# Loading q and k of the first attention tiles with one transfer each instead of two, and re-timing the first weights

## Chip, cores, metric

One core of a Trainium2 chip. The metric is the device time of one execution in microseconds (us). The kernel before takes 225.16 us (median of 5 runs, 224.05 to 225.39).

## The reference, cut to what matters

```python
# q, k, v: (4 batches, 8 heads, 768 tokens, 64)
scores = scale * q @ k^T + bias      # bias: minus slope(head) times distance
keep   = key is one of the first 8 tokens, or at most 95 tokens behind the query
a      = softmax(where(keep, scores, -1e9))
x      = (a @ v), laid out as (3072 tokens, 512)
h      = x @ w_in                    # 512 x 2048
out    = (h - tanh(h)) @ w_out       # 2048 x 512
```

## The kernel before: the parts that matter

The work is cut into 24 tiles of 128 tokens. For each tile, attention (load k, q, v; cast; transpose; scores "S"; exp "E"; "AV"; normalise; transpose of x) is followed by the MLP in two layers, `m1` (w_in) and `m2` (w_out). All attention of a tile and all MLP work share TensorE (PE). A small list scheduler inside the kernel decides the order of the instructions on each engine from estimated durations; each engine then runs its own queue in order.

```python
    PE_B = 4                 # tiles whose bias is added by a matmul; later ones are masked by VectorE
    PE_T, PE_X = 10, 10      # tiles whose transposes run on TensorE; later ones by DMA
...
    def load(u, nm, src, dst):
        ...
        if u < PE_B and nm != "vf":          # k and q of tiles 0..3: rows of 8 tokens = 2 KB
            for a in range(2):               # two transfers of 64 partitions
                started(("ld", nm, u), nc.sync.dma_start(
                    out=dst[u][a * Dh : (a + 1) * Dh].rearrange("p t d -> p (t d)"),
                    in_=rows[a * NP : (a + 1) * NP].rearrange("h (k t) d -> k h (t d)", t=H),
                ))
        else:                                # v, and later tiles: pieces of 64 numbers = 256 B
            started(("ld", nm, u), nc.sync.dma_start(out=dst[u], in_=rows.rearrange("h p d -> p h d")))
...
    WARM = (1.4, 19.0)       # filler matmuls on a zero tile keep PE busy up to here
    T_LD, T_LD8 = 1.15, 0.7  # the scheduler's idea of 256 KB in 256 B and in 2 KB pieces
    before = [ ("t", 0), ("t", 1), ("t", 2), ("t", 3), ("in", 0), ("in", 1), ("in", 2), ("in", 3), ("out", 0), ...
    # the first weight load after tiles waits for the landing of the last tile's k: w_in 0 waits for k of tile 3
```

The four quarters of w_in are called w_in_97, 98, 99 and 100, those of w_out w_out_101 to 104.

The softmax here doesn't subtract the row's maximum and nothing guards it: scores larger than these inputs give would overflow.

Of the kernel before, what the change touches and what calls it, by code (L numbers as in the profile page):

```python
# [8 lines left out]
FP32 = mybir.dt.float32  # L9
# [7 lines left out]
def kernel(  # L17
# [11 lines left out]
    nc = tc.nc  # L29

    B, H, S, Dh = q.shape
    P = 128
    NQ = S // P
    NP = H // 2
# [10 lines left out]
    WJ = 4  # L45
    FJ = CF // WJ
    NV = 8
    PE_B = 4
    PE_T, PE_X = 10, 10
    HT = 3  # L50


    EARLY, EARLY2 = 6, 4
    groups = [[u] for u in range(EARLY)] + [[u, u + 1, u + 2] for u in range(EARLY, NU, HT)]
    group_of = {u: g for g, us in enumerate(groups) for u in us}

# [77 lines left out]
    gate_of = {}  # L134
    dmas = {}

    def started(key, i):
        dmas[key] = i
        g = gate_of.get(key)
        if g is not None:  # L140
            tc.add_manual_dep(
                i.ins, dmas[g].ins.name,
                mybir.DependencyInfo(mybir.DependencyClass.Sync, mybir.DependencyReason.DATA),
                reason="order of loads",
            )


    kf, qf, vf = {}, {}, {}
    kq = {}

    def load(u, nm, src, dst):
        b, i = u // NQ, u % NQ
        dst[u] = stpool.tile([P, H, Dh], FP32, name=nm)
        rows = src[b, :, i * P : (i + 1) * P, :]
        if u < PE_B and nm != "vf":


            for a in range(2):
                started(("ld", nm, u), nc.sync.dma_start(  # L159
                    out=dst[u][a * Dh : (a + 1) * Dh].rearrange("p t d -> p (t d)"),  # L160
                    in_=rows[a * NP : (a + 1) * NP].rearrange("h (k t) d -> k h (t d)", t=H),
                ))
        else:
            started(("ld", nm, u), nc.sync.dma_start(out=dst[u], in_=rows.rearrange("h p d -> p h d")))  # L164

    def load_w_in(j):
        w = DFF // WJ
# [5 lines left out]
    def cast(u, j, src, eng):  # L173
        if u not in kq:
            kq[u] = bpool.tile([P, 2, H * Dh], BF16, name="kq")
        t = src.pop(u)
        if u < PE_B:
            eng.tensor_copy(out=kq[u][:, j, :], in_=t.rearrange("p h d -> p (h d)"))  # L178
        else:
            eng.tensor_copy(  # L180
                out=kq[u][:, j, :].rearrange("p (c a d) -> p a c d", a=2, d=Dh),
                in_=t.rearrange("p (a c) d -> p a c d", a=2),
            )
# [7 lines left out]
    def a_T(u):  # L191
        tr[u] = ps_one.tile([P, 2, NP, P], BF16, name="one")
        for j in (1, 0):
            if u < PE_B:
                for t in range(H):
                    for a in range(2):
                        r = slice(a * Dh, (a + 1) * Dh)
                        nc.tensor.transpose(
                            tr[u][r, j].rearrange("r c f -> r (c f)")[:, t * Dh : (t + 1) * Dh],
                            kq[u][r, j, t * Dh : (t + 1) * Dh], ident[r, r],  # L200
                        )
                continue
            for p in range(NP):
                nc.tensor.transpose(tr[u][:, j, p, :], kq[u][:, j, p * P : (p + 1) * P], ident)  # L204

    def a_DT(u):
        qk[u] = kpool.tile([P, 2, NP, P], BF16, name="qk")
# [10 lines left out]
    def a_Te(u, j, e):  # L218
        if u not in qk:
            qk[u] = kpool.tile([P, 2, NP, P], BF16, name="qk")  # L220
        if u < PE_B:
            copy(e, out=qk[u][:, j].rearrange("r c (k t) -> r c k t", t=H),
                 in_=tr[u][:, j].rearrange("r c f -> r (c f)").rearrange(
                     "r (t k c) -> r c k t", t=H, c=NP))
        else:
            copy(e, out=qk[u][:, j], in_=tr[u][:, j])

# [133 lines left out]
    def store(u):  # L361
        nc.sync.dma_start(out=out[u * P : (u + 1) * P, :], in_=ots.pop(u))


    AHEAD = 6.0
    WARM = (1.4, 19.0)
    T_LD, T_LD8, T_ST, T_DT, T_DX = 1.15, 0.7, 0.7, 1.75, 0.9
    T_W = {"in": 3.15, "out": 2.65}
    before = [
        ("t", 0), ("t", 1), ("t", 2), ("t", 3), ("in", 0), ("in", 1), ("in", 2), ("in", 3), ("out", 0),  # L370
        ("out", 1), ("t", 4), ("out", 2), ("out", 3), ("t", 5), ("t", 6), ("t", 7),
    ]

    def landed(it):
        return ("ld", "vf", it[1]) if it[0] == "t" else it

    tiles = [it[1] for it in before if it[0] == "t"]
    for u in range(NU):
        if u not in tiles:
            gate_of["ld", "kf", u] = ("ld", "kf", tiles[-1])  # L380
            tiles.append(u)
    for n, it in enumerate(before):
        if n and it[0] != "t" and before[n - 1][0] == "t":
            gate_of[it] = ("ld", "kf", before[n - 1][1])
        elif n >= 2 and it[0] == "t" and before[n - 1][0] != "t":
            gate_of["ld", "kf", it[1]] = landed(before[n - 2])
    prev = None
    for it in before:
        if it[0] != "t":
# [17 lines left out]
    for u in tiles:  # L407
        for nm, src, dst in (("kf", k, kf), ("qf", q, qf), ("vf", v, vf)):
            key = ("ld", nm, u)
            op(key, SP, 0.55 if u >= PE_B or nm == "vf" else 0.8, lambda u=u, nm=nm, src=src, dst=dst: load(u, nm, src, dst),  # L410
               after=[gate_of.get(key), prev and ("issue", prev)], take=[nm], dma=T_LD if u >= PE_B or nm == "vf" else T_LD8)
            prev = key
    for u in range(NU):
        i = u % NQ
        e0 = DVE if u == 0 else POOL
        c0 = 0.5 if u == 0 else 0.62
        op(("ck", u), e0, c0, lambda u=u, e=e0: cast(u, 1, kf, nc.vector if e is DVE else nc.gpsimd),
           after=[("ld", "kf", u)], take=["kq"], give=["kf"], pri=-1)
        op(("cq", u), e0, c0, lambda u=u, e=e0: cast(u, 0, qf, nc.vector if e is DVE else nc.gpsimd),
           after=[("ld", "qf", u), ("ck", u)], give=["qf"], pri=-1)  # L420
        op(("cv", u), POOL, 0.62, lambda u=u: cast_v(u),
           after=[("ld", "vf", u), ("AV", u - NV + 1) if u >= NV else None,
                  ("V", (u - NV) // NQ * NQ + NQ - 2) if u >= NV else None], give=["vf"])
        go = [key for a, key in prog if a <= u - AHEAD]
        tdep = [("ck", u), ("cq", u), ("issue", ("T", u - 1)) if u else None, go[-1] if go else None]
        if u < PE_T:
            op(("T", u), PE, 0.7 if u < PE_B else 0.46, lambda u=u: a_T(u), after=tdep, take=["one"], give=["kq"])
            for j in (1, 0):
                op(("Te", u, j), (DVE, ACT), (0.5, 0.62), lambda e, u=u, j=j: a_Te(u, j, e), after=[("T", u)])
            op(("Te", u, 2), DVE, 0.0, lambda: None, after=[("Te", u, 0), ("Te", u, 1)], give=["one"])  # L430
        else:
            op(("T", u), SP, 1.2, lambda u=u: a_DT(u), after=tdep, give=["kq"], dma=T_DT)
        te = ("Te", u, 2) if u < PE_T else ("T", u)
        for o in (0, 1) if i else (0,):
            op(("S", u, o), PE, 0.69 if u < PE_B else 0.24, lambda u=u, o=o: a_S(u, o),
               after=[te, "bias" if u < PE_B else None, ("K", u - 1) if o and i >= 2 else None], take=["big"])
            op(("E", u, o), ACT, 1.03, lambda u=u, o=o: a_E(u, o), after=[("S", u, o)],
               take=["p%d" % o], give=["big"])
            if u >= PE_B:
                op(("M", u, o), DVE, 0.73, lambda u=u, o=o: a_M(u, o),  # L440
                   after=[("E", u, o), ("mk", H - 1)])
# [40 lines left out]
    def plan():  # L482
        bufs = {"big": 2, "one": 4, "mo": 3, "kf": 4, "qf": 4, "vf": 4, "kq": 3, "p0": 3, "p1": 3,
                "x": 3, "xT": 4, "g": 3, "th": 3, "ot": 4}
        avail = {n: [0.0] * c for n, c in bufs.items()}
        free = {PE: WARM[0], ACT: 5.3, DVE: 5.1, POOL: 1.9, SP: 0.7}
        avail["one"][0] = WARM[1]
        dma_free = 0.0
        done, start = {"bias": 5.4}, {}
# [10 lines left out]
        while waiting or any(queues.values()):  # L500
# [38 lines left out]
            start[key] = t  # L539
            if o["dma"]:  # L540
                dma_free = max(dma_free, end + (1.0 if o["eng"] is SP else 1.3)) + o["dma"]
                done[key] = dma_free + 0.6
            else:
                done[key] = end + LAT[o["eng"]]
            for p in o["take"]:
# [16 lines left out]
    def with_warm(order):  # L562
        pe = sorted(t for t, key in order if ops[key]["eng"] is PE)
        last = WARM[0]
        n = 0
        for t in pe:
            us = 0.43 if t < 6.0 else 0.22
            while last + us + 0.08 <= min(t, WARM[1]):
                ops["warm", n] = dict(eng=PE, us=us, fn=warm)
                order.append((last, ("warm", n)))  # L570
                last += us
                n += 1
            last = max([last] + [t + ops[key]["us"] for u, key in order if u == t and ops[key]["eng"] is PE])
        return sorted(order, key=lambda x: x[0])

    with tc.manual_schedule(engines={PE, ACT, DVE, POOL, SP}):
        nc.vector.memset(zero, 0.0)
        make_identity(nc, ident)
        build_masks()
        for h in range(H):  # L580
            bias(h)
        for i in range(NV):
            nc.vector.memset(vb[i][:, :, Dh : Dh + 1], 1.0)
        for t, key in with_warm(order):
            ops[key]["fn"]()

# [34 lines left out]
```

## Time and profile before

| | before |
|---|---|
| median time | 225.16 us |
| span of the profiled execution (a fast one, 223.46 us) | 221.7 us |
| PE busy | 211.8 us, 96% |
| first exp | 11.91 us |
| w_in_97 issued, first used | 15.75 us, 21.56 us |
| first MLP matmul to the end of the last matmul | 21.56 to 217.86 us |

The page of the kernel before: the span, the busy times, and two rows of the span in 40 equal slices (one digit is the busy share of 5.5 us, in tenths).

```profile
span 221.7 us, 5261 instructions
PE 211.8 (96%) x2084; PEld 133.7 (60%) x2113; DVE 135.0 (61%) x278; ACT 127.5 (58%) x212; POOL 52.9 (24%) x85
...
PE   7788999999999999999999999999999999999993
...
DMA  4988998999999999999999999993621111001112
```

PE is the bound from the fifth slice to the last. What is not yet full is the first 22 us. "Busy" contains filler matmuls there, so the timeline is needed. Its columns are start and length in us, engine, line, operation, output and inputs, count, and in brackets the idle time before it and what ended that:

```profile
0.74 1.29 SPq L159 DMA_DIRECT2D kf<-in_k_dram  x2
1.20 6.22 PE L317 MATMUL one<-zero 128*128 128x512 bf16 x21 [1.20 <-DVE zero L577]
...
7.34 0.69 PE L198 MATMUL one<-ident,kq 64*64 64x64 bf16 x32
...
11.91 1.95 ACT L250 ACTIVATE pd<-big 128x1024 bf16<-128x1024 f32 x2
...
15.75 0.89 POOL L168 DMA_DIRECT2D w_in_bf_97<-in_moe_w_in_dram  x1
...
16.64 0.62 POOL L178 CAST kq<-qf 128x512 bf16<-128x512 f32 x1
...
21.56 1.08 PE L325 MATMUL one<-xT,w_in_bf_97 128*128 128x128 bf16 x16 [0.82 <-DMA w_in_bf_97<-in_moe_w_in_dram]
```

21 fillers run until 7.42 us, then tile 0's transposes; the first exp comes at 11.91 us; the first MLP matmul waits 0.82 us for w_in_97. The line at 16.64 us is the cast of tile 3's q, which landed at 15.82 us. Busy time by stretches gives the rate of the loads (columns: stretch and its length, PE busy and count, granted clock, mean busy share of the 16 DMA engines, GB/s; a share over 1 means that packets of one engine overlap in time):

```profile
2.00:6.00 4.00, 4.00 (x15) 1.00 0.78 209
6.00:10.00 4.00, 3.07 (x57) 1.00 0.95 242
10.00:14.00 4.00, 3.39 (x77) 1.00 0.86 234
```

The loads move about 235 GB/s while the engines are not quite full. (The granted clock reads 1.00 wherever the trace holds no clock record. The first record of this trace, of full clock, is at 4.29 us; the fillers before it start 0.43 us apart, those after it 0.22 us.)

### The profile page before, as it was taken

The numbers are of one execution on the slowest core, as the hardware profiler recorded it, in microseconds if no ns is written. First come the engines' busy times: TensorE is split into PE (matmuls) and PEld (weight loads), VectorE is DVE, ScalarE is ACT, GpSimd is POOL, SyncE is SP. The second block draws the span as 40 slices with busy tenths as digits, with TensorE's granted clock in tenths as the row PEclk, the third lists the DMA queues.
The fourth block names the chain that finished last, engine by engine and source line by source line (L and its number), as shares of the span: only waits on it lengthen the run. The fifth ranks groups of instructions, "written<-read, shape, count | busy, mean of one in ns | idle before, by whom it ended". The sixth has DMA issues, their size and how long they took to land.

```text
span 221.7 us, 5261 instructions
## 1 busy us (share of the span) xinstructions
PE 211.8 (96%) x2084; PEld 133.7 (60%) x2113; DVE 135.0 (61%) x278; ACT 127.5 (58%) x212; POOL 52.9 (24%) x85
## 2 busy tenths in 40 slices
PE   7788999999999999999999999999999999999993
PEld 3455897659686566566556555656656555555541
DVE  7246575456788789788886866677566444444300
ACT  5176567837689377575764666656764454534321
POOL 1468003126455453143322323321000000000000
PEclk9999999999999999999999999999999999999999
DMA  4988998999999999999999999993621111001112
GB/s 125 244 202 141 204 216 165 183 213 240 270 230 239 219 231 209 194 206 191 251 173 198 243 214 231 164 234 72 121 71 27 47 47 47 27 27 47 47 65 77
DMA packets 96409, 35.21 MB, mean 159 GB/s; under 512 B 89728, under 2 KB 91776, under 8 KB 96384
## 3 DMA queue, kind: packets, MB, share of 16 engines
q1 hardware_dynamic: 93696, 30.68, 65.5%
q0 software_dynamic: 2688, 4.19, 10.8%
q8 instruction: 16, 0.26, 0.5%
q14 instruction: 9, 0.07, 0.1%
HBM read 27.26 MB, written 6.29 MB: 151 GB/s over the span
## 4 chain that ended last, share of the span: by engine, by line
PE 85%; DMA 6%; SPq 4%; issue 2%; ACT 1%; POOL 1%; DVE 1%; POOLq 0%
PE one L325 38%; PE one L352 37%; PE big L242 5%; DMA w_in_bf_98<-in_moe_w_in_dram 4%; SPq L159 3%; PE big L265 2%; DMA vf<-in_v_dram 2%; PE big L269 2%; PE one L204 1%; PE one L292 1%; SPq L164 1%; POOL kq L178 1%; ACT pd L250 0%; DVE g L342 0%; DVE pd L254 0%
## 5 line engine op out<-in xcount | busy, mean ns | idle before, releaser
L336 ACT ACTIVATE th<-one 128x384 f32<-128x384 f32 (+1 forms) x120 | 61.3, 514 | 52.6 <-PE one L325 51.7
L342 DVE TENSOR_TENSOR g<-one,th 128x384 bf16<-128x384 f32 (+1 forms) x120 | 68.2, 581 | 38.4 <-ACT th L336 37.1
L352 PEld LDWEIGHTS <-g 128*128 128x128 bf16 x384 | 36.2, 98 | 34.3 <-issue 0.2
L180 POOL CAST kq<-kf 128x512 bf16<-128x512 f32 x20 | 13.2, 660 | 72.0 <-DMA kf<-in_k_dram 69.1
L250 ACT ACTIVATE pd<-big 128x1024 bf16<-128x1024 f32 x24 | 24.5, 1025 | 9.9 <-PE big L242 9.8
L325 PE MATMUL one<-xT,w_in_bf_97 128*128 128x128 bf16 (+1 forms) x192 | 25.5, 273 | 0.8 <-DMA w_in_bf_97<-in_moe_w_in_dram 0.8
L325 PE MATMUL one<-xT,w_in_bf_98 128*128 128x128 bf16 (+1 forms) x192 | 25.5, 273 | 0.2 <-DMA w_in_bf_98<-in_moe_w_in_dram 0.2
L325 PE MATMUL one<-xT,w_in_bf_99 128*128 128x128 bf16 (+1 forms) x192 | 25.6, 273 | 0.0
L325 PE MATMUL one<-xT,w_in_bf_100 128*128 128x128 bf16 (+1 forms) x192 | 25.2, 273 | 0.1
L352 PE MATMUL one<-w_out_bf_101,g 128*128 128x512 bf16 x89 | 24.1, 379 | 0.5 <-DVE qk L216 0.2
L359 ACT COPY ot<-one 128x512 f32<-128x512 f32 x24 | 14.1, 588 | 16.9 <-PE one L352 16.7
L352 PE MATMUL one<-w_out_bf_103,g 128*128 128x512 bf16 x90 | 23.5, 379 | 0.3
L352 PE MATMUL one<-w_out_bf_104,g 128*128 128x512 bf16 x89 | 23.3, 379 | 0.5 <-issue 0.2
L352 PE MATMUL one<-w_out_bf_102,g 128*128 128x512 bf16 x90 | 23.4, 379 | 0.3
L254 DVE TENSOR_TENSOR pd<-pd,mk 128x1024 bf16<-128x1024 bf16 x20 | 15.4, 771 | 10.2 <-ACT pd L250 9.9
L250 ACT ACTIVATE po<-big 128x1024 bf16<-128x1024 f32 x20 | 20.5, 1027 | 0.5 <-PE big L242 0.5
L325 PEld LDWEIGHTS <-w_in_bf_97 128*128 128x128 bf16 x192 | 16.1, 114 | 7.0 <-DMA w_in_bf_97<-in_moe_w_in_dram 0.9
L325 PEld LDWEIGHTS <-w_in_bf_100 128*128 128x128 bf16 x192 | 16.3, 113 | 6.4 <-issue 0.2
L325 PEld LDWEIGHTS <-w_in_bf_99 128*128 128x128 bf16 x192 | 16.2, 114 | 6.5
L325 PEld LDWEIGHTS <-w_in_bf_98 128*128 128x128 bf16 x192 | 16.0, 114 | 6.5 <-DMA w_in_bf_98<-in_moe_w_in_dram 0.3
L278 DVE TENSOR_TENSOR x<-big,rden 128x512 bf16<-128x512 f32 x24 | 16.6, 692 | 0.9
L180 POOL CAST kq<-qf 128x512 bf16<-128x512 f32 x20 | 14.2, 711 | 8.2 <-DMA qf<-in_q_dram 8.1
(100 smaller groups left out, 189.3 us busy)
## 6 DMA issues: line engine op xcount, KB each, us to landing
vf<-in_v_dram SPq DMA_DIRECT2D x24, 256.0 KB, 4.5
out_dram<-ot SPq DMA_DIRECT2D x24, 256.0 KB, 2.7
kf<-in_k_dram SPq DMA_DIRECT2D x20, 256.0 KB, 3.6
qf<-in_q_dram SPq DMA_DIRECT2D x20, 256.0 KB, 4.3
kf<-in_k_dram SPq DMA_DIRECT2D x8, 128.0 KB, 3.6
qf<-in_q_dram SPq DMA_DIRECT2D x8, 128.0 KB, 3.4
w_in_bf_97<-in_moe_w_in_dram POOLq DMA_DIRECT2D x1, 512.0 KB, 5.8
w_in_bf_98<-in_moe_w_in_dram POOLq DMA_DIRECT2D x1, 512.0 KB, 8.1
```

Source lines behind the costliest of these rows:

```text
L159: started(("ld", nm, u), nc.sync.dma_start(out=dst[u][a * Dh : (a + 1) * Dh].rearrange("p t d -> p (t d)"), in_=rows[a * NP : (a + 1) * NP ...
L180: eng.tensor_copy(out=kq[u][:, j, :].rearrange("p (c a d) -> p a c d", a=2, d=Dh), in_=t.rearrange("p (a c) d -> p a c d", a=2),)
L242: nc.tensor.matmul(s[:, hh * NP + p, :], qk[u - o][r, 1, p, :], qk[u][r, 0, p, :], start=(u >= PE_B), stop=(u >= PE_B or p == NP - 1),)
L250: nc.scalar.activation(pr[u, o], s, AF.Exp, bias=0.0, scale=scale)
L254: nc.vector.tensor_tensor(out=pr[u, o], in0=pr[u, o], in1=mk[:, :, m, :], op=ALU.mult)
L265: nc.tensor.matmul(dst, pr[u, 0][:, h, :], vb[u % NV][:, h, :], start=True, stop=last,)
L278: nc.vector.tensor_tensor(out=xs[u].rearrange("q (a h) d -> q a h d", a=2), in0=t[:, :, :, 0:Dh], in1=rden.to_broadcast([P, 2, H // 2, Dh] ...
L325: nc.tensor.matmul(t[:, (f - f0) * n : (f - f0 + 1) * n], w_in_bf[j][:, c, i : FJ * P : FJ], xT[b][:, c, o : o + n], start=(c == 0), stop= ...
L336: nc.scalar.activation(h_view(ths[g, f0], g), h_view(hs[g, f0], g), AF.Tanh, bias=0.0, scale=1.0)
L342: nc.vector.tensor_tensor(out=gs[b][:, f0 : f0 + m, o : o + n], in0=h_view(hs.pop((g, f0)), g), in1=h_view(ths.pop((g, f0)), g), op=ALU.su ...
L352: nc.tensor.matmul(os_[u], gs[u // HT][:, f, t * P : (t + 1) * P], w_out_bf[f // FJ][:, f % FJ, :], start=(f == 0), stop=(f == CF - 1),)
L359: nc.scalar.copy(out=ots[u], in_=os_.pop(u))
```

## The change

The intent was to have PE at useful work earlier. k and q of tiles 0 to 3 become one transfer of 128 partitions each, so SyncE needs less time to issue them; the first q is issued by ScalarE; the transposes use columns of the identity matrix as the moving operand, so k and q each get their own PSUM tile and copy; casts of the first tiles may go to VectorE; the first weight load is gated by a computed schedule of the transfers (w_in_97 then waits for q of tile 2 instead of k of tile 3), w_out_101 comes second; some counts of tiles move.

```diff
-    PE_B = 4
-    PE_T, PE_X = 10, 10
-    EARLY, EARLY2 = 6, 4
+    PE_B = 5
+    LB = 4
+    PE_T, PE_X = 9, 9
+    EARLY, EARLY2 = 6, 6
...
+    BY_ACT = [("qf", 0)]
+        eng = nc.scalar if (nm, u) in BY_ACT else nc.sync
-            for a in range(2):
-                started(("ld", nm, u), nc.sync.dma_start(... 64 partitions ...))
+            started(("ld", nm, u), eng.dma_start(
+                out=dst[u].rearrange("p t d -> p (t d)"),
+                in_=rows.rearrange("h (k t) d -> k h (t d)", t=H),
+            ))
...
+    def a_TL(u, j):
+        tr[u, j] = ps_one.tile([P, NP * P], FP32, name="one")
+        for t in range(H):
+            for a in range(2):
+                nc.tensor.matmul(
+                    tr[u, j][a * Dh : (a + 1) * Dh, t * Dh : (t + 1) * Dh],
+                    kq[u][:, j, t * Dh : (t + 1) * Dh],
+                    ident.rearrange("p (k a c) -> p a k c", a=2, c=NP)[:, a], start=True, stop=True,
+                )
...
-    AHEAD = 6.0
-    WARM = (1.4, 19.0)
+    AHEAD = 4.5
+    WARM = (1.3, 16.0)
-        ... ("t", 3), ("in", 0), ("in", 1), ("in", 2), ("in", 3), ("out", 0),
+        ... ("t", 3), ("in", 0), ("out", 0), ("in", 1), ("in", 2), ("in", 3),
+    T_LAND, T_SP, T_POOL = 1.0, 1.6, 2.2        # gates: the last load that ends early enough
+            due = at + 0.3 - T_LAND - (T_SP if it[0] == "t" else T_POOL)
+            past = [key for e, key in ends if e <= due]
+            if past:
+                gate_of[first] = past[-1]
... (cut)
```

More of the change, by code (lines that the diff above doesn't have):

```diff
@@ L154, in load @@
         rows = src[b, :, i * P : (i + 1) * P, :]
-        if u < PE_B and nm != "vf":
-            for a in range(2):
-                started(("ld", nm, u), nc.sync.dma_start(
-                    out=dst[u][a * Dh : (a + 1) * Dh].rearrange("p t d -> p (t d)"),
-                    in_=rows[a * NP : (a + 1) * NP].rearrange("h (k t) d -> k h (t d)", t=H),
-                ))
+        eng = nc.scalar if (nm, u) in BY_ACT else nc.sync
+        if u < LB and nm != "vf":
+            started(("ld", nm, u), eng.dma_start(
+                out=dst[u].rearrange("p t d -> p (t d)"),
+                in_=rows.rearrange("h (k t) d -> k h (t d)", t=H),
+            ))
         else:
-            started(("ld", nm, u), nc.sync.dma_start(out=dst[u], in_=rows.rearrange("h p d -> p h d")))
+            started(("ld", nm, u), eng.dma_start(out=dst[u], in_=rows.rearrange("h p d -> p h d")))
     def load_w_in(j):
@@ L176, in cast @@
         t = src.pop(u)
-        if u < PE_B:
+        if u < LB:
             eng.tensor_copy(out=kq[u][:, j, :], in_=t.rearrange("p h d -> p (h d)"))
@@ L193, in a_T @@
         for j in (1, 0):
-            if u < PE_B:
-                for t in range(H):
-                    for a in range(2):
-                        r = slice(a * Dh, (a + 1) * Dh)
-                        nc.tensor.transpose(
-                            tr[u][r, j].rearrange("r c f -> r (c f)")[:, t * Dh : (t + 1) * Dh],
-                            kq[u][r, j, t * Dh : (t + 1) * Dh], ident[r, r],
-                        )
-                continue
             for p in range(NP):
                 nc.tensor.transpose(tr[u][:, j, p, :], kq[u][:, j, p * P : (p + 1) * P], ident)
+    def a_TL(u, j):
[7 more added lines that the diff above has]
+                )
     def a_DT(u):
@@ L220, in a_Te @@
             qk[u] = kpool.tile([P, 2, NP, P], BF16, name="qk")
-        if u < PE_B:
+        if u < LB:
             copy(e, out=qk[u][:, j].rearrange("r c (k t) -> r c k t", t=H),
-                 in_=tr[u][:, j].rearrange("r c f -> r (c f)").rearrange(
-                     "r (t k c) -> r c k t", t=H, c=NP))
+                 in_=tr.pop((u, j)).rearrange("r (t k c) -> r c k t", t=H, c=NP))
         else:
@@ L369 @@
     before = [
-        ("t", 0), ("t", 1), ("t", 2), ("t", 3), ("in", 0), ("in", 1), ("in", 2), ("in", 3), ("out", 0),
+        ("t", 0), ("t", 1), ("t", 2), ("t", 3), ("in", 0), ("out", 0), ("in", 1), ("in", 2), ("in", 3),
         ("out", 1), ("t", 4), ("out", 2), ("out", 3), ("t", 5), ("t", 6), ("t", 7),
     ]
-    def landed(it):
-        return ("ld", "vf", it[1]) if it[0] == "t" else it
     tiles = [it[1] for it in before if it[0] == "t"]
+    T_LAND, T_SP, T_POOL = 1.0, 1.6, 2.2
+    ends = []
+    at = 2.3
+    for n, it in enumerate(before):
+        first = ("ld", "kf", it[1]) if it[0] == "t" else it
+        if n and (it[0] == "t") != (before[n - 1][0] == "t"):
+            due = at + 0.3 - T_LAND - (T_SP if it[0] == "t" else T_POOL)
+            past = [key for e, key in ends if e <= due]
+            if past:
+                gate_of[first] = past[-1]
+        if it[0] == "t":
+            for nm in ("kf", "qf", "vf"):
+                at += T_LD if it[1] >= LB or nm == "vf" else T_LD8
+                ends.append((at, ("ld", nm, it[1])))
+        else:
+            at += T_W[it[0]]
+            ends.append((at, it))
     for u in range(NU):
@@ L381 @@
             tiles.append(u)
-    for n, it in enumerate(before):
-        if n and it[0] != "t" and before[n - 1][0] == "t":
-            gate_of[it] = ("ld", "kf", before[n - 1][1])
-        elif n >= 2 and it[0] == "t" and before[n - 1][0] != "t":
-            gate_of["ld", "kf", it[1]] = landed(before[n - 2])
     prev = None
@@ L409 @@
             key = ("ld", nm, u)
-            op(key, SP, 0.55 if u >= PE_B or nm == "vf" else 0.8, lambda u=u, nm=nm, src=src, dst=dst: load(u, nm, src, dst),
-               after=[gate_of.get(key), prev and ("issue", prev)], take=[nm], dma=T_LD if u >= PE_B or nm == "vf" else T_LD8)
+            by_act = (nm, u) in BY_ACT
+            op(key, SP, 0.0 if by_act else 0.62,
+               (lambda: None) if by_act else lambda u=u, nm=nm, src=src, dst=dst: load(u, nm, src, dst),
+               after=[gate_of.get(key), prev and ("issue", prev)], take=[nm], dma=T_LD if u >= LB or nm == "vf" else T_LD8)
             prev = key
@@ L414 @@
         i = u % NQ
-        e0 = DVE if u == 0 else POOL
-        c0 = 0.5 if u == 0 else 0.62
-        op(("ck", u), e0, c0, lambda u=u, e=e0: cast(u, 1, kf, nc.vector if e is DVE else nc.gpsimd),
+        e0, c0 = ((DVE, POOL), (0.48, 0.62)) if u < PE_B else ((POOL,), (0.62,))
+        op(("ck", u), e0, c0, lambda e, u=u: cast(u, 1, kf, nc.vector if e is DVE else nc.gpsimd),
            after=[("ld", "kf", u)], take=["kq"], give=["kf"], pri=-1)
-        op(("cq", u), e0, c0, lambda u=u, e=e0: cast(u, 0, qf, nc.vector if e is DVE else nc.gpsimd),
+        op(("cq", u), e0, c0, lambda e, u=u: cast(u, 0, qf, nc.vector if e is DVE else nc.gpsimd),
            after=[("ld", "qf", u), ("ck", u)], give=["qf"], pri=-1)
@@ L424 @@
         go = [key for a, key in prog if a <= u - AHEAD]
-        tdep = [("ck", u), ("cq", u), ("issue", ("T", u - 1)) if u else None, go[-1] if go else None]
-        if u < PE_T:
-            op(("T", u), PE, 0.7 if u < PE_B else 0.46, lambda u=u: a_T(u), after=tdep, take=["one"], give=["kq"])
+        before_T = [("issue", ("T", u - 1)) if u else None, go[-1] if go else None]
+        tdep = [("ck", u), ("cq", u)] + before_T
+        if u < LB:
+            for j, c in ((1, "ck"), (0, "cq")):
+                op(("T", u, j), PE, 0.44, lambda u=u, j=j: a_TL(u, j), after=[(c, u)] + before_T, take=["one"])
+                op(("Te", u, j), (DVE, ACT), (0.7, 0.6), lambda e, u=u, j=j: a_Te(u, j, e), after=[("T", u, j)],
+                   give=["one"])
+            op(("Te", u, 2), DVE, 0.0, lambda: None, after=[("Te", u, 0), ("Te", u, 1)])
+            op(("T", u), PE, 0.0, lambda: None, after=[("T", u, 0), ("T", u, 1)], give=["kq"])
+        elif u < PE_T:
+            op(("T", u), PE, 0.46, lambda u=u: a_T(u), after=tdep, take=["one"], give=["kq"])
             for j in (1, 0):
@@ L434 @@
         for o in (0, 1) if i else (0,):
-            op(("S", u, o), PE, 0.69 if u < PE_B else 0.24, lambda u=u, o=o: a_S(u, o),
+            op(("S", u, o), PE, 0.72 if u < PE_B else 0.24, lambda u=u, o=o: a_S(u, o),
                after=[te, "bias" if u < PE_B else None, ("K", u - 1) if o and i >= 2 else None], take=["big"])
@@ L485, in plan @@
         avail = {n: [0.0] * c for n, c in bufs.items()}
-        free = {PE: WARM[0], ACT: 5.3, DVE: 5.1, POOL: 1.9, SP: 0.7}
+        free = {PE: WARM[0], ACT: 5.2, DVE: 4.6, POOL: 1.9, SP: 0.7}
         avail["one"][0] = WARM[1]
@@ L541, in plan @@
                 dma_free = max(dma_free, end + (1.0 if o["eng"] is SP else 1.3)) + o["dma"]
-                done[key] = dma_free + 0.6
+                done[key] = dma_free + 1.0
             else:
@@ L566, in with_warm @@
         for t in pe:
-            us = 0.43 if t < 6.0 else 0.22
-            while last + us + 0.08 <= min(t, WARM[1]):
+            while True:
+                us = 0.43 if last < 4.8 else 0.22
+                if last + us + 0.08 > min(t, WARM[1]):
+                    break
                 ops["warm", n] = dict(eng=PE, us=us, fn=warm)
@@ L576 @@
     with tc.manual_schedule(engines={PE, ACT, DVE, POOL, SP}):
+        for nm, u in BY_ACT:
+            load(u, nm, {"kf": k, "qf": q, "vf": v}[nm], {"kf": kf, "qf": qf, "vf": vf}[nm])
         nc.vector.memset(zero, 0.0)
+        for i in range(NV):
+            nc.vector.memset(vb[i][:, :, Dh : Dh + 1], 1.0)
+        build_masks()
         make_identity(nc, ident)
-        build_masks()
         for h in range(H):
             bias(h)
-        for i in range(NV):
-            nc.vector.memset(vb[i][:, :, Dh : Dh + 1], 1.0)
         for t, key in with_warm(order):
```

## The prediction

> **What bounds the kernel now.** TensorE. The page gives PE 211.8 us busy of a 221.7 us span; the chain of waits lies 85% on PE. By stretches of busy time: from 21.56 us (first MLP matmul, line 325) to 217.90 us PE idles only 2 us; 3.8 us of tail follow. What can be won lies before 21.56 us: there PE idles about 4 us, and some 7.4 us of its "busy" are filler matmuls on the zero tile (24). Useful work there is about 10 us.
>
> The first MLP matmul waits (0.82 us in the timeline) for w_in_97: issued at 15.75 us, packets from 17.3, landed at 21.56. It is gated on tile 3's k, and the tile loads are fed by SyncE's queue: 3.1 us of issuing a tile (two half-loads of 0.6 us each for k and q, one for v). The second limit stands close: attention of tile 2 ends at 20.7 us.
>
> **What the change does.**
> - k and q of tiles 0-3 become one load each, and the first q goes by ScalarE: SP issues 1.9 us per tile instead of 3.1. Then packets limit: in this trace's packet records a 2 KB packet takes 84 ns of one engine, a 256 B one 18 ns, so 256 KB cost about 0.7 us (k, q) and 1.15 us (v) over 16 engines, 2.55 us a tile. The Trainium skill, "DMA: Bandwidth & Descriptors", Specifications, asks for at least 512 B for line rate; the trace agrees (24 against 14 GB/s per engine). Estimate: tile 3's q is in at 11.5 to 12 us instead of about 16.
> - w_in_97 is gated on q of tile 2 (landing about 9.5 us): issued about 9.7, landed about 16.6 us. w_out_101 is put second, so w_in_98/99/100 come about 22.4/25.3/28 us instead of 25.36/27.8/30.5.
> - Transposes of k and q get separate PSUM tiles and copies, so k starts before q; casts of tiles 0-4 go partly to VectorE; fewer fillers stand before T(0), which 21 fillers held to 7.34 us although q was cast at 6.1. I expect the first exp near 8.1 us instead of 11.91. From there ScalarE (exps of 1.03 us, copies of 0.58) sets the pace: attention of tile 2 ends at about 17.3 us.
> - Tile 4 gets its bias by matmul: PE pays about 1.1 us more (a score block 0.86 against 0.28 us); tile 9 loses PE transposes, about 0.7 us. Net +0.4 us on PE, on the critical path.
>
> **Sum.** First MLP matmul at about 17.3 us, 4.2 us earlier, now by attention, not the load. The following weights are 2 to 3 us earlier, and one early m2 quarter and one MLP quarter of tile 3 fill holes, so I expect the end of tiles 0-2's first MLP layer about 4.4 us earlier in terms of work done. Minus 0.4 us PE work, minus about 0.3 us because an early m2 holds one of four PSUM banks for 10 us: 3.7 us. Predicted 221.2 us, 8 in 10 between 219.3 and 223.2. Chances: faster by over 2% 0.32, within 2% 0.66, slower 0.02.
>
> **What would show it.** Timeline: first line-327 matmul at 16.5 to 18 us; first exp at about 8 us; w_in_97 issued before 11 us; tile 0-3 loads all issued by about 8 us; zero-tile matmuls 14. Windows: PE idle between the first MLP matmul and 50 us under 1.5 us. Tail unchanged.
>
> **What would make it wrong.** 2 KB packets slower than 84 ns beside 256 B ones (their mean was 112 ns): loads 1 to 2 us later. Waits for w_in_98 or 99, or PSUM banks, giving 1 us or more back. A PE clock cold for longer. Fewer PE stalls after 50 us would carry it past 2%.

## The result

| | before | after |
|---|---|---|
| median time, 5 runs each | 225.16 us (224.05 to 225.39) | 222.64 us (221.96 to 223.04) |
| ratio | | 0.9891, 95% interval 0.9857 to 0.9924 |
| span, profiled execution | 221.7 us | 220.2 us |
| first exp | 11.91 us | 10.91 us (predicted 8.1) |
| first MLP matmul | 21.56 us | 20.28 us (predicted 17.3) |
| from there to the end of the last matmul | 196.30 us | 196.24 us |

A ratio is the mean time of one kernel's fast runs over that of the other's of the same rounds, so it is not quite the ratio of the medians quoted. The change gains 1.1%, about 2.5 us; 3.7 us were predicted, and 221.2 us against 222.64 us measured.

The page of the changed kernel:

```profile
span 220.2 us, 5240 instructions
PE 212.4 (96%) x2092; PEld 132.2 (60%) x2092; DVE 133.3 (61%) x276; ACT 128.7 (58%) x215; POOL 49.2 (22%) x79
...
PE   5899999999999999999999999999999999999993
...
DMA  6999999899999999999999999965134121001112
```

PE is full from the third slice instead of the fifth, and the DMA engines are at 90% or more in nearly every slice from the second to the 25th. The timeline of the changed kernel, for the lines shown above:

```profile
0.74 0.67 SPq L160 DMA_DIRECT2D kf<-in_k_dram  x1
...
5.82 0.61 POOL L179 CAST kq<-kf 128x512 bf16<-128x512 f32 x1 [4.12 <-DMA kf<-in_k_dram]
...
6.48 1.07 PE L203 MATMUL one<-ident,kq 128*64 128x64 bf16 x32 [2.12 <-POOL kq L179]
...
7.48 2.31 PE L319 MATMUL one<-zero 128*128 128x512 bf16 x5
...
10.91 1.02 ACT L252 ACTIVATE pd<-big 128x1024 bf16<-128x1024 f32 x1 [2.68 <-PE big L244]
...
12.65 0.89 POOL L169 DMA_DIRECT2D w_in_bf_97<-in_moe_w_in_dram  x1 [1.65 <-DMA qf<-in_q_dram]
...
15.66 0.43 DVE L179 CAST kq<-qf 128x512 bf16<-128x512 f32 x1 [0.55 <-DMA qf<-in_q_dram]
...
20.28 1.08 PE L327 MATMUL one<-xT,w_in_bf_97 128*128 128x128 bf16 x16
```

Tile 0's k is cast only at 5.82 us (4.97 before). Five fillers then stand between tile 0's transposes and its scores, at 0.43 us each where 0.22 was planned: PE still ran at half clock, for the first clock record of this trace, of full clock, comes only at 10.30 us. "A PE clock cold for longer" is one of the risks that the prediction names. Tile 3's q is cast at 15.66 us; it landed at 15.64 us, 0.2 us earlier than before. w_in_97 is issued 3.1 us earlier than before. The list of transfers of the changed kernel (KB, us from issue to landing) says when it landed:

```profile
w_in_bf_97<-in_moe_w_in_dram POOLq DMA_DIRECT2D x1, 512.0 KB, 7.6
w_out_bf_101<-in_moe_w_out_dram POOLq DMA_DIRECT2D x1, 512.0 KB, 9.2
w_in_bf_98<-in_moe_w_in_dram POOLq DMA_DIRECT2D x1, 512.0 KB, 11.2
```

12.65 + 7.6 = 20.25 us: w_in_97 lands as tile 2's AV matmuls end, so two limits meet at the first MLP matmul. The stretches of the changed kernel show why the loads are no sooner:

```profile
2.00:6.00 4.00, 2.36 (x6) 1.00 1.05 226
6.00:10.00 4.00, 3.52 (x38) 1.00 1.16 233
10.00:14.00 4.00, 3.50 (x93) 1.00 1.16 241
```

The engines are now oversubscribed (1.16 where it was 0.95 and 0.86), but the bytes per second are the same. In the packet records the 2 KB packets take 136 to 138 ns in the median from 6 to 14 us (84 ns before), and the 256 B ones about 25 (18 before).

One caution in reading PE's busy time: the profile of the kernel before lacks 26 of the 384 records of its m2 matmuls, that of the change none; those of b0_again, p1_tiles, i2_plan and n2_nov_fill lack 25 or 26. A missing record can look like a wait of up to 0.2 us for "issue". So not the idle time but the length of the stretch from the first MLP matmul (F) to the end of the last matmul (E) is compared below; it is called L. The profile of the change is that of one of its two fastest executions (221.97 us), so a stall that comes and goes could be missing from it too.

### The profile page after: what moved, and what is told of

Same layout as the page of the kernel before. It is cut to its first block, busy times and chain, and to the rows that moved or that the text cites. A ratio compares the mean times of both kernels' runs of the same rounds, so it can differ in the third digit from the quotient of the medians.

```text
span 220.2 us, 5240 instructions
## 1 busy us (share of the span) xinstructions
PE 212.4 (96%) x2092; PEld 132.2 (60%) x2092; DVE 133.3 (61%) x276; ACT 128.7 (58%) x215; POOL 49.2 (22%) x79
## 4 chain that ended last, share of the span: by engine, by line
PE 94%; DMA 2%; ACT 1%; DVE 0%; POOL 0%; issue 0%
PE one L327 39%; PE one L354 38%; PE big L244 6%; PE big L267 3%; DMA kf<-in_k_dram 2%; PE big L271 2%; PE big L237 2%; PE one L319 1%; PE one L203 1%; PE one L196 1%; PE one L294 1%; ACT pd L252 0%; DVE g L344 0%; POOL kq L179 0%; ACT th L338 0%; ACT ot L361 0%
## 5 line engine op out<-in xcount | busy, mean ns | idle before, releaser
L327 PE MATMUL one<-xT,w_in_bf_100 128*128 128x128 bf16 (+1 forms) x192 | 25.7, 274 | 0.0
L327 PE MATMUL one<-xT,w_in_bf_99 128*128 128x128 bf16 (+1 forms) x192 | 25.2, 274 | 0.0
L327 PE MATMUL one<-xT,w_in_bf_98 128*128 128x128 bf16 (+1 forms) x192 | 24.8, 273 | 0.3 <-DVE g L344 0.3
L327 PE MATMUL one<-xT,w_in_bf_97 128*128 128x128 bf16 (+1 forms) x192 | 24.7, 274 | 0.0
L354 PE MATMUL one<-w_out_bf_101,g 128*128 128x512 bf16 x96 | 24.7, 380 | 0.0
L354 PE MATMUL one<-w_out_bf_103,g 128*128 128x512 bf16 x96 | 24.7, 380 | 0.0
L354 PE MATMUL one<-w_out_bf_102,g 128*128 128x512 bf16 x96 | 24.7, 380 | 0.0
L354 PE MATMUL one<-w_out_bf_104,g 128*128 128x512 bf16 x96 | 24.6, 379 | 0.0
L256 DVE TENSOR_TENSOR pd<-pd,mk 128x1024 bf16<-128x1024 bf16 x19 | 14.6, 768 | 11.5 <-ACT pd L252 11.3
L181 POOL CAST kq<-kf 128x512 bf16<-128x512 f32 x19 | 12.2, 643 | 40.0 <-DMA kf<-in_k_dram 24.0
L280 DVE TENSOR_TENSOR x<-big,rden 128x512 bf16<-128x512 f32 x24 | 16.6, 692 | 0.8
L244 PEld LDWEIGHTS <-qk 64*128 64x128 bf16 x352 | 9.9, 94 | 10.8 <-issue 9.4
```

Source lines behind the costliest of these rows:

```text
L181: eng.tensor_copy(out=kq[u][:, j, :].rearrange("p (c a d) -> p a c d", a=2, d=Dh), in_=t.rearrange("p (a c) d -> p a c d", a=2),)
L244: nc.tensor.matmul(s[:, hh * NP + p, :], qk[u - o][r, 1, p, :], qk[u][r, 0, p, :], start=(u >= PE_B), stop=(u >= PE_B or p == NP - 1),)
L256: nc.vector.tensor_tensor(out=pr[u, o], in0=pr[u, o], in1=mk[:, :, m, :], op=ALU.mult)
L280: nc.vector.tensor_tensor(out=xs[u].rearrange("q (a h) d -> q a h d", a=2), in0=t[:, :, :, 0:Dh], in1=rden.to_broadcast([P, 2, H // 2, Dh] ...
L327: nc.tensor.matmul(t[:, (f - f0) * n : (f - f0 + 1) * n], w_in_bf[j][:, c, i : FJ * P : FJ], xT[b][:, c, o : o + n], start=(c == 0), stop= ...
L354: nc.tensor.matmul(os_[u], gs[u // HT][:, f, t * P : (t + 1) * P], w_out_bf[f // FJ][:, f % FJ, :], start=(f == 0), stop=(f == CF - 1),)
```

## The experiments

Each ran 5 rounds beside the kernel before (b0 included). "Against the change" is the difference of the two ratios to the kernel before, times 225 us; the intervals of the ratios are about 0.4% wide to either side, so below some 1 us such a difference is weak.

| run | ratio to before (95%) | against the change | first exp | F | L |
|---|---|---|---|---|---|
| change | 0.9891 (0.9857 to 0.9924) | | 10.91 | 20.28 | 196.24 |
| a1_fill | 0.9918 (0.9881 to 0.9956) | +0.6 us | 8.43 | 20.74 | 196.21 |
| a2_ring | 0.9992 (0.9954 to 1.0030) | +2.3 us | 10.73 | 22.91 | 196.23 |
| a3_both | 1.0022 (0.9992 to 1.0053) | +2.9 us | 8.50 | 23.88 | 196.21 |
| a4_halves | 0.9883 (0.9854 to 0.9913) | -0.2 us | 10.68 | 20.45 | 196.37 |
| n1_nov | 0.9845 (0.9803 to 0.9888) | -1.0 us | 10.13 | 19.42 | 197.29 |
| n2_nov_fill | 0.9827 (0.9779 to 0.9875) | -1.4 us | 8.93 | 19.02 | 196.36 |
| u1_gate | 0.9926 (0.9891 to 0.9961) | +0.8 us | 10.15 | 20.55 | 197.01 |
| p1_tiles | 0.9942 (0.9904 to 0.9980) | +1.1 us | 8.89 | 20.73 | 197.73 |
| i1_order | 0.9971 (0.9931 to 1.0012) | +1.8 us | 9.84 | 17.73 | 202.58 |
| i2_plan | 0.9962 (0.9923 to 1.0000) | +1.6 us | 8.37 | 20.77 | 197.84 |
| c1_early | 0.9980 (0.9930 to 1.0029) | (on before) | 11.58 | 23.35 | 196.64 |
| b0_again | 1.0011 (0.9973 to 1.0050) | (is before) | 11.50 | 21.64 | 198.33 |

All but n1 and n2 give the right result. In a1, a2, a3, a4, n1, n2 and u1 the scheduler's order is that of the change and only the named thing is edited; p1, i1 and i2 let the scheduler plan again.

### a1_fill: the fillers

```diff
-  7 fillers before tile 0's transposes, 5 between them and its scores
+  14 fillers before tile 0's transposes, none between
```

> The changed kernel with its filler matmuls moved: 14 before the first transpose (7 in the change), none between it and the first scores (5 in the change). Filler theory (PE went cold and 5 fillers of 0.43 us stood before the first scores): first exp at about 8.8 us instead of 10.91, and, if that is what delays the MLP, the first MLP matmul at 18.5 us or earlier and 1.5 to 2 us less in all. Load theory (the tile loads still come at some 235 GB/s, so w_in_97, gated on them, lands at 20.25 us whatever attention does): first exp earlier as well, but the first MLP matmul stays at 20.2 to 20.4 us behind w_in_97, and the time moves by less than 0.7 us.

The timeline of this run:

```profile
8.43 1.02 ACT L252 ACTIVATE pd<-big 128x1024 bf16<-128x1024 f32 x1 [0.49 <-PE big L244]
...
11.05 0.43 DVE L179 CAST kq<-kf 128x512 bf16<-128x512 f32 x1 [1.21 <-DMA kf<-in_k_dram]
11.53 0.44 PE L203 MATMUL one<-ident,kq 128*64 128x64 bf16 x16 [1.43 <-DVE kq L179]
...
13.24 1.02 ACT L252 ACTIVATE pd<-big 128x1024 bf16<-128x1024 f32 x1 [0.64 <-PE big L244]
```

The first exp came 2.5 us earlier, as predicted for fillers and a cold PE. Most of that is the clock and not the place of the fillers. In p1_tiles (below) five fillers stand in the same place, and the first exp comes at 8.89 us:

```profile
6.83 1.25 PE L319 MATMUL one<-zero 128*128 128x512 bf16 x5
```

There the trace has full clock from 4.71 us and the five fillers take 1.25 us; in the change it has full clock only from 10.30 us and they take 2.31 us.

Nothing came of the earlier exp: tile 1's exp moved only from 13.71 to 13.24 us, and F came 0.46 us later. In the queues of PE and ScalarE, tile 2's k transpose and its copy stand ahead of tile 1's scores and exp, and tile 2's k landed only at 11 us. A second cause lies in the clock, as the stretches of a1_fill show:

```profile
11.00:12.00 1.00, 0.47 (x17) 1.00 1.32 209
12.00:13.00 1.00, 1.00 (x10) 0.62 1.22 248
13.00:14.00 1.00, 1.00 (x24) 0.50 1.03 246
14.00:15.00 1.00, 1.00 (x5) 0.50 1.25 230
```

After PE had waited for that k, its clock was half from 12.25 to 15.66 us by the trace's record, while it was busy throughout. An estimate from this record: half of 3.4 us, so up to 1.7 us of PE's time. All six executions of a1_fill have a mean clock of 0.985 to 0.992, where only one of the change's five is that low (0.990). So this run does not say what the fillers alone do to F. It does show that they alone could not bring the 18.5 us of the filler theory, since w_in_97 landed at 12.42 + 7.5 = 19.9 us.

### a2_ring and a3_both: two queues for the loads

```diff
-    BY_ACT = [("qf", 0)]
+    BY_ACT = [("qf", 0), ("qf", 1), ("qf", 2), ("qf", 3)]     # k and v stay on SyncE
+    gate of w_in_97: k of tile 2
```

a3_both has this edit and the one of a1 (14 fillers first, none later).

> The changed kernel with q of tiles 0 to 3 all issued first on ScalarE's queue, k and v on SyncE's, w_in_97 gated on k of tile 2; order of all else as in the change. Theory 1 (one backlogged queue delivers only about 235 GB/s, two deliver more, as the 326 GB/s between 3 and 4 us in the trace of the change): 2 KB packets near 85 to 100 ns instead of 130 to 150, over 290 GB/s from 2 to 10 us, tile 3's k and q in before 13 us (15.6), w_in_97 landing 2 us earlier or more. Theory 2 (a limit common to both queues, memory or engines): 235 to 250 GB/s as before, tile loads end at 15.5 to 16.2 us. The time in either: at most 1 us less, as attention (first exp about 10.9 us) stays as it is.

> Both of the two edits above. If the two limits stand one behind the other (attention and w_in_97 both ready at 20.2 us) and two queues do deliver more: first MLP matmul at 17 to 18.3 us and 2 to 3 us less than the change. If the load rate is common to both queues: first MLP matmul not before 19.8 us, the time within 0.7 us of the change's.

The stretches of a2_ring, and below them its timeline line of tile 1's k:

```profile
2.00:6.00 4.00, 2.36 (x6) 1.00 1.02 232
6.00:10.00 4.00, 3.84 (x39) 1.00 1.12 242
10.00:14.00 4.00, 2.13 (x61) 0.97 1.23 233
```

```profile
10.78 0.43 DVE L180 CAST kq<-kf 128x512 bf16<-128x512 f32 x1 [5.83 <-DMA kf<-in_k_dram]
```

232 to 242 GB/s: the rate is common to both queues, theory 2. The 325 GB/s seen between 3 and 4 us in the change came in a2_ring too (336 GB/s), and fell to 251 in the next microsecond although both queues still held only 2 KB packets; it belongs to the start, not to having two queues. The Trainium skill says the same of queues in general: "Trainium Kernel Development and Optimization", Key Constraints, has transfers of all issuing queues run on the same 16 DMA engines and interleave, so that issuing from several only saves the issue time. This trace agrees. The edit even lost 2.3 us, which was not expected: the four q loads took half of the rate, k of tile 1 was cast at 10.78 us instead of 7.97, and attention waited. PE's clock has a share in the loss that was not separated: by the traces' records it was half from 13.78 to 17.19 us in a2_ring and from 12.38 to 19.21 us in a3_both, and the one execution of a2_ring with a mean clock of 0.999 took 223.26 us, the other five, at 0.984 to 0.990, 224.56 to 225.34 us. a3_both agrees on the rate: first exp at 8.50 us, yet w_in_97 landed at 20.0 us (20.25 in the change) and F came at 23.88, far from the 17 to 18.3 us that two faster queues would have given. With a fixed rate, the order in which bytes come is all that issuing can change.

### a4_halves: the single loads undone

```diff
-            one transfer of 128 partitions for each k and q of tiles 0..3
+            for a in range(2): one transfer of 64 partitions each
```

> The changed kernel with each k and q load of tiles 0 to 3 split again in two loads of 64 partitions (ScalarE issues both halves of the first q). Prediction's theory (issuing on SyncE, 3.1 us a tile, was the limit of the loads): tile 3's k and q land 1.5 us later or more, the time goes up 1 us or more. Load rate theory (the rate is near 235 GB/s in both, so single loads bought little): tile 3's q lands within 0.7 us of 15.6 us and the time moves by less than 0.7 us.

The stretches of a4_halves:

```profile
2.00:6.00 4.00, 2.36 (x6) 1.00 1.03 239
6.00:10.00 4.00, 3.81 (x39) 1.00 1.00 249
10.00:14.00 4.00, 3.50 (x96) 1.00 1.07 245
```

The rate is the same or a little higher, tile 3's q is cast at 16.29 us (15.66), and the time is that of the change. So the headline of the change, one load in place of two, is worth nothing measurable here. SyncE's 3.1 us of issuing per tile looked like the limit because the rate of the transfers, 0.79 MB per tile at 235 GB/s = 3.3 us, happens to be the same length.

### n1_nov and n2_nov_fill: fewer bytes, and a square of two causes

```diff
+        if nm == "vf" and 1 <= u <= 3: return        # v of tiles 1..3 is not loaded
-    cast_v reads the tile's own v
+    cast_v of tiles 1..3 reads tile 0's v            # wrong result on purpose
```

n2 adds the filler edit of a1.

> Wrong on purpose: the changed kernel without the v loads of tiles 1, 2 and 3 (their v is tile 0's), so 0.79 MB of the first 3.1 MB less to load; all else in the order of the change. Load theory (tile loads come at about 240 GB/s, and attention and w_in_97 hang on them): k of tile 2 lands about 2 us earlier (9.4 to 10 us), q of tile 3 about 3 us earlier, w_in_97 lands near 18 us, first MLP matmul at 17.8 to 18.8 us instead of 20.28, and 1.3 to 2.5 us less than the change (about 220.5 us). Filler theory (first exp at 10.9 us because of fillers and the cold PE sets the pace): first exp and first MLP matmul stay where they are, within 0.6 us, and so does the time.

> Wrong on purpose, the fourth corner of a square: the changed kernel with the fillers moved as in a1 and without the v loads of tiles 1 to 3 as in n1. First MLP matmul was at 20.28 us (change), 20.74 (fillers alone), 19.42 (v loads alone). If loads and fillers are two chains of nearly equal length, so that each alone hides behind the other: 17 to 18.3 us for both together, and 2 to 3 us less than the change (219.6 to 220.6 us). If the sum of the single effects is all there is: 19.2 to 20 us and at most 1.2 us less than the change.

With 0.79 MB less to load, F came 0.86 us earlier in n1, with the fillers where they were; F missed the expected 17.8 to 18.8 us. The time fell by about 1 us in n1 and 1.4 us in n2, at the edge of what the intervals resolve. w_in_97 landed at 16.9 us in both (11.12 + 5.8 in n1, 11.43 + 5.5 in n2), long before F: there F waits for attention alone and no longer for the weights. Of F, fillers alone gave +0.46 us, fewer bytes alone -0.86, both -1.26. With the bytes gone the filler edit went from useless to worth 0.4 us. That would fit two chains that stand partly behind each other, but it is not shown: the profile of a1 has its stretch of half clock and those of n1 and n2 have none after 9.05 and 6.41 us. And n2 was expected at 17 to 18.3 us and came at 19.02. A stretch of n2 shows that the k and q loads are still slow (the v packets are gone from it after 7 us):

```profile
6.00:10.00 4.00, 3.29 (x78) 1.00 1.06 249
```

In its packet records, 2 KB packets alone in flight on one queue take 134 ns and bring 254 to 260 GB/s from 7 to 11 us; one 256 KB load lands every 1.0 us. The slow packets are thus not a matter of 256 B pieces beside them.

### u1_gate and c1_early: the gate of the first weights

```diff
 u1 (on the change):   gate of w_in_97: k of tile 3 again, instead of q of tile 2
 c1 (on the kernel before): gate of w_in_97: q of tile 2, and its issue moved ahead of the cast of that q on GpSimd
```

> The changed kernel with w_in_97 gated on k of tile 3 again, as in the kernel before, instead of q of tile 2; all else in its order. If the earlier gate is what the change gained by: w_in_97 is issued about 2 us later (14.7), lands at 21.3 us or later, first MLP matmul at 21.3 us or later and 0.8 to 1.6 us more than the change. If the transfers are a full pipe either way (weights and tile 3's loads share the engines), w_in_97 lands within 0.5 us of 20.25 and the time moves by less than 0.5 us.

> The kernel before with one part of the change alone: w_in_97 gated on q of tile 2 and issued on GpSimd's queue before the cast of tile 2's q, not after tile 3's k. If the gate is what the change gained by: w_in_97 lands at 20 to 20.6 us instead of 21.56, first MLP matmul at 20.7 to 20.9 us (behind attention of tile 2), 0.6 to 1.4 us less than the kernel before. If the gain came from the other parts: less than 0.4 us of change, or a loss from tile 3's loads being pushed back.

u1: F moved by 0.27 us only, but PE then waited 0.49 us for w_out_101, and the time rose by about 0.8 us, at the edge of what the intervals resolve. The gate of q of tile 2 is worth roughly that. c1: the same gate put on the kernel before gained nothing. The timeline of c1_early, tile 3's q:

```profile
19.42 0.61 POOL L178 CAST kq<-qf 128x512 bf16<-128x512 f32 x1 [3.47 <-DMA qf<-in_q_dram]
```

Tile 3's q, which was cast at 16.64 us in the kernel before, now kept GpSimd waiting until 19.42 us, and F came at 23.35 us in this profile. The first packets of w_in_97 come at 14.3 us in this trace, before that q has landed (19.30 us; 15.82 in the kernel before), so w_in_97 probably took the rate from tile 3; this is read from one trace. In the change SyncE has issued all of tile 3's loads by 10.0 us, ahead of the weights; why exactly that spares them was not tested.

### p1_tiles and b0_again: after the first MLP matmul

```diff
 p1 (on the change): PE_B = 4; PE_T, PE_X = 10, 10      # planned again
 b0: the kernel before, unchanged
```

> The changed kernel with its counts of tiles put back: bias by matmul for tiles 0 to 3 only (tile 4 masked by VectorE again), transposes on TensorE up to tile 9. Prediction's term: PE work of the tiles was +0.4 us in the change, so undoing it gives 0.2 to 0.6 us less time if PE stays full, and the first MLP matmul stays within 0.3 us of 20.28. Rival (tile 4's bias on PE saved VectorE and ScalarE work that PE would have waited for): 0.3 us or more longer.

> The kernel before once more, for a second profile and the noise of the ratio. Its first profile (span 221.7 us, 223.46 us in that execution) was faster than all its timed runs (224.05 to 225.39). Ratio within 0.4% of 1; the second profile's span is expected nearer 223 us. If PE's clock state or the loads of the first 22 us differ from run to run, the first MLP matmul comes 0.5 us or more later than 21.56; if not, the difference lies after it.

Undoing the counts did not save 0.2 to 0.6 us, it cost about 1.1 us, at the edge of what the intervals resolve; L went from 196.24 to 197.73 us and F from 20.28 to 20.73. (This profile has half clock from 11.53 to 14.95 us, which may be what moved F. The 1.1 us are not that: the two executions with a mean clock of 1.0 took 223.44 and 223.54 us, the three at 0.992 took 223.19 to 224.26.) The waits of PE in p1_tiles after 50 us (engine and line, released by: us in total, times, longest):

```profile
PE one L354 <- issue: 0.8, 5, 0.2
PE big L271 <- DVE po L256: 0.5, 1, 0.5
```

The first line is the holes of missing records. The second is a stall of 0.5 us, on VectorE's mask; the rest of the 1.5 us in L was not located. The second profile of the kernel before explains why stalls after F were missed. Its span is 223.8 us, F is the same within 0.1 us, and L is 198.33 us instead of 196.30. The waits of PE in b0_again:

```profile
PE big L242 <- DMA qk<-kq: 0.8, 1, 0.8
...
PE one L204 <- POOL kq L180: 0.5, 1, 0.5
...
PE one L352 <- DVE qk L216: 0.3, 1, 0.3
```

The first two lie after 50 us, on a transpose by DMA (77.67 us in the timeline) and on a cast ahead of a PE transpose (50.65 us). The first profile of the kernel before had fallen on an execution without them: 223.46 us, faster than every one of its first five timed runs. The change has none of these in its profile, and the runs that kept its order have L = 196.2 to 196.4 us, whatever their F (19.02 to 23.88 us), but for u1, where PE waited 0.5 us for w_out_101, and n1 (197.29), where it waited 1.0 us for two transposes by DMA: in these profiles such stalls are rarer with the change's order, but it does not rule them out. The 1.1 us of p1 and the 1.5 us in L point the same way, but the first is weak as a difference of ratios and the second comes from one profile, of p1's second slowest execution of six. Since p1 was planned anew, it tests the counts together with the order that follows from them.

### i1_order and i2_plan: two tries at better

```diff
 both: T_LD, T_LD8 = 1.1, 1.07 instead of 1.15, 0.7 (measured in backlog)
 i1: order tile 0, 1, 2, w_in 0, tile 3, w_in 1, w_out 0, w_in 2, ...
 i2: order kept; gate q of tile 2; fillers as in a1
```

> A try at better: the changed kernel with its scheduler told 1.07 and 1.1 us per 256 KB load (measured in backlog) instead of 0.7 and 1.15, and the order tile 0, 1, 2, w_in 0, tile 3, w_in 1, w_out 0, w_in 2, ... If the total rate of loads is the limit and PE only has to have work earlier: w_in_97 lands at 16.5 to 17.5 us, first MLP matmul before 18 us, 1 to 2.5 us less than the change (220 to 221.5 us). If tile 3's later landing costs attention as much as the earlier weights give: within 0.7 us of the change.

> A try at better: the changed kernel with its scheduler told the measured 1.07 and 1.1 us per 256 KB load, its order of loads kept, w_in_97 gated on q of tile 2, and 14 fillers before the first transpose, none between it and the first scores. ScalarE then does both exps of tile 1 before it copies tile 2's transposes, so tile 1 no longer waits for tile 2's k. If the coupling through in-order queues costs: attention of tile 2 ends before 19.8 us, first MLP matmul at 20.0 to 20.4 us (w_in_97), time 0 to 1 us less than the change. If loads alone set the pace: within 0.5 us of it.

Both missed. i1 did bring the first MLP matmul to 17.73 us, but tile 3's q was cast at 19.72 us and PE stood idle for 1.2 us between 21 and 26 us; in all it lost what it had won, and more. i2 had F at 20.77 us and L at 197.84: its new plan brought back a stall of 0.5 us (at 138 us, behind ScalarE), and the rest of the 1.6 us in L was not located. The change itself stays the best correct version that ran (a4_halves equals it).

## Why the prediction was right, and where its steps were off

- **Range and direction: right.** 222.64 us lies within 219.3 to 223.2, "within 2%" was the likeliest class, and about half of the gain of 2.5 us came where it was sought, at the start of the span. But that the number fell inside the range is partly luck: two wrong terms worked against each other, too large a gain before F, and a loss after F where about 1.2 us were gained.
- **"2 KB packets cost 84 ns, 2.55 us a tile": wrong, the largest term.** 84 ns was the median packet of a stretch in which the engines were not full. With the queue full the median was 136 to 138 ns, and in n2, where k and q come alone, a 256 KB load took 1.0 us where 0.7 was predicted. From tile 1 on, a tile's k or q landed 2.9 to 3.6 us after that of the tile before in the kernel before, and 3.2 to 3.3 us in the change, not 2.55; tile 3's q landed at 15.64 us (predicted: 11.5 to 12; before: 15.82), w_in_97 landed at 20.25 us (predicted 16.6). The prediction names this as its first risk ("their mean was 112 ns") and then sums with the median. The mean would have been nearer.
- **"SyncE's issuing is the limit of the loads": wrong.** a4_halves brings the second issue back and loses nothing; a2_ring adds a queue and the rate stays.
- **"First exp near 8.1 us": wrong, 10.91.** k of tile 0 was cast at 5.82 us, and PE's clock was half until 10.30 us, so five fillers ran at 0.43 us in front of the scores and the bias matmul behind them was slow too. With full clock from 4.71 us, p1_tiles has 8.89 us with the fillers in place; a1_fill, without them, 8.43 us. The chain after it was well sized: 9.4 us from the first exp to F, where the prediction has 9.2. But a1_fill shows that this chain is no fixed length: start it earlier and it waits for tile 2's k.
- **"First MLP matmul at 17.3 us, by attention and not the load": off by 3.0 us.** q of tile 2 landed at 12.34 us (predicted: about 9.5), and from there to F it took 7.9 us, where the prediction has 7.8: in this profile the late loads alone make up the miss. n1 and n2 show that fewer bytes move F; the filler edit helped only in n2, where there were fewer bytes and no stretch of half clock.
- **"Net +0.4 us on PE" and "-0.3 us for PSUM banks": no such loss was seen.** Counted in the two traces, the change has 4 bias matmuls more after F (216 ns apart) and 12 transposes fewer (56 ns apart), so about 0.2 us more work. Yet L did not grow: 196.24 us against 196.30 and 198.33, and undoing the counts, and with them the order, costs about 1.1 us. The prediction's own last sentence, that fewer PE stalls after 50 us would help, fits this: the two profiles of the kernel before differ by such stalls, and the single one that the prediction had hid them. The PSUM term was not tested by itself.

So the gain has two parts. F comes 1.28 to 1.36 us earlier (against the two profiles of before). L in the kernel before was 196.30 us in one profile and 198.33 in another, and is 196.24 in the change: 0.06 to 2.1 us. 1.3 us from F and about 1.2 us from L make the 2.5 us measured; the second number is what the first leaves over, not a measurement of its own.

Some things stay open. What limits these loads to about 235 to 260 GB/s was not found; two queues, half-size transfers and leaving out the 256 B packets do not lift it. n2 still has F at 19.02 us; how much of the rest down to 17.3 us is the still slow k and q loads and how much the order in the engines' queues was not separated. Nor was it tested what a1, a2 and a3 would give without their stretches of half clock. What in p1 costs the 1.1 us, a count or the order that follows from it, was not separated either.

## What to carry to other kernels

Before speeding up the issue of transfers, compare the bytes per second of the stretch with the same stretch under a full queue; a packet's shortest or median time in a half-idle stretch is not its cost in a full one, while bytes per second was the same in both. When the rate is fixed, only the order of the bytes can be won, and moving one load forward pushes another back (a2, c1, i1). Read the clock of every stretch that is compared, and check it by the spacing of like matmuls: a1, a2 and a3 each hold 3.4 to 6.8 us of half clock after 12 us, and the change none. Take two profiles of the kernel before when its runs scatter by more than the effect sought: stalls that come and go are part of what a change can win.

## What the Trainium skill lacked or had wrong

- "DMA: Bandwidth & Descriptors", Bandwidth, measures 341 GB/s for a 1 MB load on one other path (SWDGE) and gives about 358 GB/s as the memory's limit for one core. What no page has is the rate of many 256 KB loads in 2 KB and 256 B pieces, queued one behind the other: here about 235 GB/s, and 254 to 260 GB/s and 134 ns a packet where the 2 KB pieces come alone (n2_nov_fill), against an 84 ns median when the engines were not full. Its rule of at least 512 B for line rate, used in the prediction, is no promise of that rate.
- No page says that a packet's recorded time is longer when more loads are queued. The DMA share of 10 to 14 us went from 0.86 to 1.16 at 234 and 241 GB/s, so here the share did not measure the rate left.
- "TensorE: Matmul & The Clock Gate", Part 1, says that the first 3.4 us or so of matmul work run at half clock and that the moment varies from run to run. The traces agree that it varies, more widely than that number: under fillers without a gap, full clock is on record 3.1 us after the first filler in the kernel before and 5.2 us in n2_nov_fill. In the change, whose first fillers end at 4.36 us, it is on record only at 10.30 us; with the same first fillers p1_tiles has it at 4.71 us, and the same five later fillers took 2.31 us in the change and 1.25 us in p1_tiles.
